# Loading the first batch's tokens and first matrix in the order TensorE uses them, by halves, with fewer warm-up products

## The chip, the cores and the metric

The kernel runs on one core of one Trainium2 chip. The metric is the device time of one execution, in microseconds (us). The core has five engines that run their own instruction streams: TensorE (PE, with its weight loads shown apart as PEld), VectorE (DVE), ScalarE (ACT), GpSimd (POOL) and SyncE (SP). Loads and stores are issued by SP, ACT and POOL and are carried by sixteen DMA engines that all three share.

## The reference

Two blocks follow each other, on 8 batches of 3008 tokens of 256 channels. The first multiplies the tokens' spectrum by a filter, the second is a feed-forward layer:

```
X = np.fft.rfft(x, axis=1)
F = (filt_r + 1j * filt_i)[None, :, :]
y = np.fft.irfft(X * F, n=x.shape[1], axis=1)     # (8, 3008, 256)

x = y.reshape(8 * 3008, 256)
h = x @ w_in                                      # (24064, 2048)
g = h - np.tanh(h)
out = g @ w_out                                   # (24064, 256)
```

## The kernel before, in words

The sequence of 3008 tokens is written as 64 times 47: token 47 q + r, with q from 0 to 63 and r from 0 to 46. The Fourier transform is done as two steps of small matrix products, one over q (for each r) and one over r. Because r and 47 - r go together, the kernel puts the 64 tokens of r on partitions 0 to 63 and the 64 tokens of 47 - r on partitions 64 to 127, for r from 0 to 23. The feed-forward layer then takes nearly all of the time: from about 80 us on, TensorE runs one product after another until the end, while the transforms of the later batches are threaded between them.

The change lies in the prologue, which handles batch 0 alone. The order of the instructions is the order of the code (the pool is opened with a manual schedule). What happens there, with the lines of the kernel before:

- Three token tiles `xs[0]`, `xs[1]`, `xs[2]` (128 partitions, 8 rows of r, 256 channels, 1 MB each) are loaded, each in four pieces: the lower 64 partitions ("low", L1181) and the upper 64 ("high", L1184), for rows 0 to 3 (k = 0) and 4 to 7 (k = 4). A low piece is 64 runs of 4 KB. A high piece goes backwards through the tokens, so it is made of runs of 1 KB. Row 0 of the upper half of `xs[0]` is set to zero instead of loaded.
- Three pieces `fh` of the first matrix `f` (128 partitions by 512 columns, 256 KB each) are loaded at L1177, one for each token tile. VectorE writes each into the tile `f0` twice, as it is (L1188) and times a column of signs (L1189).
- `warmer` (L1081) makes TensorE multiply a tile of ones with itself, 15 products, before the first real product. Each 4-byte product is two instructions in the trace.
- `first0(c)` (L1071) does the first step for token tile c: for each pair of rows four products of 128 by 128 into one bank, which ScalarE (in two places VectorE) copies out (L1074):

```
def first0(c):
    for i in range(0, 8, 2):
        r = 8 * c + i
        pf = z0("pf", [128, 2, 2, 128])
        for h in range(2):
            for k in range(2):
                nc.tensor.matmul(pf[:, h, k], xs[c][:, i + k, h * 128:h * 128 + 128],
                                 f0[:, r + k], start=True, stop=True)
        copy = V.tensor_copy if c == 2 and i % 4 else ACT.copy
        copy(turnt[:, :, :, r:r + 2], pf.rearrange("p h k n -> p h n k"))
```

- After the third `first0` come the transposes (`pq`, L1094), the second step (`pa` and `pb`, L428), the product with the filter on VectorE (L447 to L456), the way back (`pe`, L1139 and L1141), the stores of its result to DRAM (`ct`, L1145 and L483) and a load of these as `e` (L1129). The first product of the main part, `pu` (L595), needs that load.
- The filters of the first two groups are loaded by GpSimd at L1122. A one-element copy named `gate` (L1197) stands ahead of them on GpSimd and reads an element of `xs[2]`, so that they are issued only when that piece has landed. GpSimd clears three small parts of the filter tiles (L1195).
- The tiles `one` (L1191) and the first part of `mats` (L1192), needed from `pq` and `pa` on, and the first piece `raw` of the weights (L175) are loaded by SP behind its token pieces.

SP and ACT hand their loads out over eight completion semaphores in turn, in the order of the program: each load waits, on the engine that issues it, until the load eight before it on these two queues has landed. GpSimd has eight of its own.

Of the kernel before, what the change touches and what calls it, by code (L numbers as in the profile page):

```python
# [9 lines left out]
F32 = mybir.dt.float32  # L10
# [5 lines left out]
ALU = mybir.AluOpType  # L16

BATCH, SEQ, DM = 8, 3008, 256
NQ, NR = 64, 47
NA = NQ // 2  # L20
NH = (NR + 1) // 2
SG = 5
# [95 lines left out]
def kernel(  # L118
# [9 lines left out]
    nc = tc.nc  # L128
    V, G, ACT = nc.vector, nc.gpsimd, nc.scalar
    f_d, both_d, g_d, whole_d, mats_d, one_d, wide_d, pairs_d, whole_pairs_d, split_d = (  # L130
        nc.inline_tensor(v, name=n).ap()
        for v, n in zip(_consts(), ("f", "f_both", "g", "g_whole", "mats", "one", "wide",
                                    "g_pairs", "g_whole_pairs", "f_split")))
# [12 lines left out]
    def dram(t, off, dims):  # L146
        return bass.AP(tensor=t, offset=off, ap=[list(d) for d in dims])
# [478 lines left out]
    def merged(U):  # L626

        i, u = divmod(U, 4)
        b, c = groups[i]
        return u == 2 and (1 < c < NC - 1 if b == 0 else  # L630
                           c < (4 if b == BATCH - 2 else NC) and b < BATCH - 1)
# [400 lines left out]
    with tc.tile_pool(name="tr", bufs=2) as tr, tc.manual_schedule():  # L1032
# [16 lines left out]
        with tc.tile_pool(name="pro", bufs=1) as pro, \  # L1049
                tc.tile_pool(name="ps0", bufs=8, space=bass.MemoryType.PSUM) as ps0:  # L1050

            def z0(name, shape):
                return ps0.tile(shape, F32, tag="z", bufs=8, name=name)
# [3 lines left out]
            def big(shape, dtype, name):  # L1057

                return pro.tile(shape, dtype, tag="big", bufs=3, name=name)
# [4 lines left out]
# [12 lines that stand above are left out]
            def warmer(n, t=None):  # L1076

                warm = z0("warm", [128, 256])
                t = f0[:, 0:2].rearrange("p a n -> p (a n)") if t is None else t
                for _ in range(n):  # L1080
                    nc.tensor.matmul(warm, t[:, 0:128], t, start=True, stop=True)  # L1081
# [31 lines left out]
            def filters_of(g):  # L1113

                t, queue = filt[g % 3], G if g < 2 else nc.sync
                if g == last_g:
                    t = pro.tile([128, 512], I64, tag="raw", bufs=3, name="filt_end")
                    t = t.bitcast(F32).rearrange("p (v n) -> p v n", v=4)
                    ACT.mul(t[0:HB], f0.rearrange("p a n -> p (a n)")[0:HB, 0:4 * DM]
                            .rearrange("p (v n) -> p v n", v=4), 0.0)  # L1120
                for v, row, n, src in filter_rows(g):
                    queue.dma_start(t[row:row + n, v], src)  # L1122
                return t
# [38 lines left out]
            filt = [pro.tile([KM, 4, DM], F32, name=f"filt{k}") for k in range(3)]  # L1162
            f0 = pro.tile([128, NH, 128], F32, name="f0")
# [3 lines left out]
            sgn = cst.tile([128, 1], F32, name="sgn")  # L1167
            for half in range(2):
                V.memset(sgn[64 * half:64 * half + 64], 1.0 - 2 * half)
            V.memset(filt[2][:, 0], 1.0)  # L1170
            xs, began = [], []
            for c in range(3):
                lo = int(c == 0)
                xt = big([128, 8, DM], F32, "x0")
                xs.append(xt)
                fh = pro.tile([128, 8, 64], F32, tag="e1", bufs=4, name="fh")
                (ACT if c else nc.sync).dma_start(fh, f_d[:, 512 * c:512 * c + 512])  # L1177
                if lo:
                    V.memset(xt[64:128, 0], 0.0)
                for k in (0, 4):  # L1180
                    nc.sync.dma_start(xt[0:64, k:k + 4], dram(x.tensor, (8 * c + k) * DM,  # L1181
                                                              [[NR * DM, 64], [1, 4 * DM]]))
                    at = max(k, lo)
                    (ACT if c + k == 0 else G).dma_start(  # L1184
                        xt[64:128, at:k + 4], dram(x.tensor, (NR - 8 * c - at) * DM,
                                                   [[NR * DM, 64], [-DM, k + 4 - at], [1, DM]]))
                r = 8 * c
                V.tensor_copy(f0[:, r:r + 8, 0:64], fh)  # L1188
                V.tensor_scalar(out=f0[:, r:r + 8, 64:128], in0=fh,  # L1189
                                scalar1=sgn, scalar2=None, op0=ALU.mult)  # L1190
            nc.sync.dma_start(one, one_d)  # L1191
            nc.sync.dma_start(mats[:, 0:3 * KM], mats_d[:, 0:3 * KM])  # L1192
            ACT.activation(warm_b, warm_b, AF.Arctan)
            for t in filt:
                G.memset(t[0:SG, 2:4], 0.0)  # L1195
            gate = cst.tile([1, 1], F32, name="gate")
            G.tensor_copy(gate, xs[2][64:65, 0, 0:1])  # L1197
            fts = {0: filters_of(0)}

            warmer(15, filt[2][:, 0])  # L1200
            first0(0)
            first0(1)
            began.append(begun(tiles0, jobs[0], queue=nc.sync))
# [107 lines left out]
        with tc.tile_pool(name="dn", bufs=2) as dn, \  # L1311
# [73 lines left out]
            for U in range(total + 2):  # L1385
# [8 lines left out]
                if U < total:  # L1394
                    p, c = groups[i]
                    if c == 0 and u == 0 and 0 < p < BATCH - 1:
                        plan += STAGES
                    at = (2, 0) if merged(4 * i + 2) else (3, 2)
# [124 lines left out]
```

## Time and profile before

| what | value |
|---|---|
| median of three runs | 2543.22 us (2541.65 to 2544.98) |
| the profiled execution | 2542.18 us |
| its span, first to last instruction | 2540.3 us |
| PE busy in the span | 2522.6 us (99%) |
| DVE, ACT, POOL busy | 1935.6, 1694.2, 1532.0 us |
| granted TensorE clock, mean | 0.999 |

The profile is of one execution. The span is 1.9 us shorter than that execution's time; the rest lies around it. A row of the timeline gives the start, the duration, the engine, the line, the operation and how many instructions it merges; in brackets stands the idle time ahead of it and what ended it. ACTq and SPq are the instruction queues of ACT and SP, on which DMA issues stand. The rows for DMA queues name q1 for SP's loads, q10 for ACT's and q0 for GpSimd's, with the count of packets, the megabytes and the share of the sixteen engines' time.

### The profile page before, as it was taken

Reading aid. Unit: us, or ns where it says so; the run is one execution under the profiler, and the core shown is the slowest. Engines: PE = TensorE matmul, PEld = TensorE weight load, DVE = VectorE, ACT = ScalarE, POOL = GpSimd, SP = SyncE. Lnnn points to the kernel's source line nnn. Section 1 sums busy time; section 2 is a strip of 40 time slices with the busy share of each in tenths; the row PEclk is TensorE's granted clock in tenths of the full one; section 3 lists DMA queues with packets and bytes.
Section 4 is the critical chain, followed back from the end, with each engine's and each line's share of the span. In section 5 each row is a group of like instructions: output and inputs, shape, how many; then the busy total and the mean of one; then the engine's idle time right before and its main releaser. Section 6 shows DMA issues by size and latency. Waiting matters only on the chain.

```text
span 2540.3 us, 44575 instructions
## 1 busy us (share of the span) xinstructions
PE 2522.6 (99%) x17072; PEld 2173.1 (86%) x17072; DVE 1935.6 (76%) x2270; ACT 1694.2 (67%) x2551; POOL 1532.0 (60%) x1112
## 2 busy tenths in 40 slices
PE   9999999999999999999999999999999999999998
PEld 8678889888898888988888888898889888898887
DVE  6888877988678876888669886698866888555555
ACT  4666666667666766676667666666666666666665
POOL 5255665667556765676656665666655666455552
PEclk9999999999999999999999999999999999999999
DMA  9854224422343323342334322343123322110110
GB/s 245 261 150 117 65 54 100 112 65 53 86 108 91 82 69 89 80 112 59 80 87 105 87 56 72 96 111 89 36 72 84 92 66 53 26 31 19 25 22 19
DMA packets 333664, 211.37 MB, mean 83 GB/s; under 512 B 231645, under 2 KB 305531, under 8 KB 329793
## 3 DMA queue, kind: packets, MB, share of 16 engines
q1 hardware_dynamic: 319091, 184.93, 29.8%
q0 software_dynamic: 11120, 16.16, 2.3%
q10 hardware_dynamic: 3230, 7.34, 0.9%
q8 instruction: 136, 2.23, 0.4%
q14 instruction: 87, 0.71, 0.1%
HBM read 127.81 MB, written 83.39 MB: 83 GB/s over the span
## 4 chain that ended last, share of the span: by engine, by line
PE 96%; DVE 2%; DMA 1%; issue 0%; POOL 0%; ACT 0%; ACTq 0%; SPq 0%; POOLq 0%; DVEq 0%
PE o L821 44%; PE x L648 25%; PE z L648 12%; PE y L648 6%; PE pm L415 2%; PE pu L595 2%; PE pm L351 1%; PE o L883 1%; PE pf L308 1%; DMA filt<-in_filt_r_dram 1%; DMA x<-in_x_dram 0%; DMA ct<-e 0%; PE o L719 0%; PE x L719 0%; PE z L719 0%
## 5 line engine op out<-in xcount | busy, mean ns | idle before, releaser
L821 PE MATMUL o<-t,wd 128*128 128x256 f32 (+1 forms) x3008 | 762.7, 376 | 0.0
L619 POOL TENSOR_TENSOR t<-h 128x512 f32<-128x512 f32 (+1 forms) x184 | 303.6, 1650 | 707.3 <-DVE h L771 642.2
L771 DVE TENSOR_TENSOR h<-h,y 128x1024 f32<-128x1024 f32 (+1 forms) x384 | 571.0, 1487 | 156.4 <-ACT y L767 156.4
L821 PEld LDWEIGHTS o<-t,wd 128*128 128x128 f32 x3008 | 568.8, 190 | 84.5 <-POOL o L853 15.1
L648 PE MATMUL x<-tu,wu 128*128 128x256 f32 (+1 forms) x2256 | 571.4, 376 | 0.0
L821 PE MATMUL o<-h,wd 128*128 128x256 f32 (+1 forms) x2256 | 569.9, 375 | 0.2 <-DVE h L771 0.2
L648 PEld LDWEIGHTS x<-tu,wu 128*128 128x128 f32 x2256 | 427.4, 190 | 53.8 <-issue 3.9
L821 PEld LDWEIGHTS o<-h,wd 128*128 128x128 f32 x2256 | 428.3, 190 | 50.9 <-issue 0.8
L654 ACT COPY s<-x 128x512 f32<-128x512 f32 (+1 forms) x188 | 109.3, 581 | 517.4 <-PE x L648 517.3
L764 ACT ACTIVATE y<-y 128x1024 f32<-128x1024 f32 (+1 forms) x384 | 399.5, 1040 | 12.1
L767 ACT ACTIVATE y<-y 128x1024 f32<-128x1024 f32 (+1 forms) x384 | 399.8, 1041 | 4.6
L761 ACT ACTIVATE y<-h 128x1024 f32<-128x1024 f32 (+1 forms) x384 | 400.6, 1043 | 2.5 <-DVE h L697 1.7
L622 POOL TENSOR_TENSOR t<-h,t 128x512 f32<-128x512 f32 (+1 forms) x184 | 338.3, 1838 | 0.0
L620 POOL TENSOR_TENSOR t<-h,t 128x512 f32<-128x512 f32 (+1 forms) x184 | 310.5, 1688 | 14.4
L621 POOL TENSOR_TENSOR t<-h 128x512 f32<-128x512 f32 (+1 forms) x184 | 276.9, 1505 | 0.0
L654 ACT COPY u<-x 128x512 f32<-128x512 f32 (+1 forms) x376 | 214.1, 569 | 72.9 <-PE x L648 69.6
L697 DVE COPY h<-x 128x512 f32<-128x512 f32 (+1 forms) x188 | 127.6, 679 | 129.1 <-PE x L648 128.9
L689 DVE TENSOR_TENSOR h<-z,u 128x512 f32<-128x512 f32 (+1 forms) x188 | 127.2, 677 | 88.9 <-ACT u L654 88.5
L648 PE MATMUL x<-ut,wu 128*128 128x256 f32 (+1 forms) x752 | 194.0, 380 | 0.2 <-DVE h L697 0.2
L648 PE MATMUL z<-tu,wu 128*128 128x256 f32 (+1 forms) x752 | 190.2, 375 | 1.4 <-DVE h L705 1.4
L648 PE MATMUL y<-ut,wu 128*128 128x256 f32 (+1 forms) x752 | 190.1, 375 | 0.0
L648 PE MATMUL z<-ut,wu 128*128 128x256 f32 (+1 forms) x752 | 190.0, 375 | 0.0
(215 smaller groups left out, 2933.5 us busy)
## 6 DMA issues: line engine op xcount, KB each, us to landing
ft<-filt SPq DMA_DIRECT2D x28, 1024.0 KB
ct<-nn SPq DMA_DIRECT2D x56, 512.0 KB
e<-ct SPq DMA_DIRECT2D x47, 512.0 KB
a<-ct SPq DMA_DIRECT2D x112, 192.0 KB
out_dram<-ot SPq DMA_DIRECT2D x1248, 16.0 KB
x_sb<-in_x_dram SPq DMA_DIRECT2D x110, 128.0 KB
ct<-a SPq DMA_DIRECT2D x60, 128.0 KB
ct<-x_sb SPq DMA_DIRECT2D x60, 128.0 KB
```

Of the source, the lines that this page charges most:

```text
L619: by.tensor_sub(t[0], b[0][1], b[0][0])
L620: by.tensor_sub(t[1], b[1][1], t[0])
L621: by.tensor_sub(t[2], b[1][1], b[0][1])
L622: by.tensor_sub(t[3], b[1][0], t[1])
L648: nc.tensor.matmul(bank[:, k], wu[:, q - 1, (2 * u + k) * 128:(2 * u + k + 1) * 128], rhs[q - 1], start=(first and k == 0), stop=True, ski ...
L654: ACT.copy(t, X)
L697: V.tensor_copy(h[:, 2, :, 0:w], X)
L761: ACT.activation(y[k], ht[k], AF.Arctan, scale=TURN)
L764: ACT.activation(y[k], y[k], AF.Tanh, scale=BEND)
L767: ACT.activation(y[k], y[k], AF.Square, scale=SCALE, accum_out=y_sums[:, 2 * U + k // 2:2 * U + k // 2 + 1])
L771: V.tensor_mul(ht[k], ht[k], y[k])
L821: nc.tensor.matmul(product(q), wd[:, q - 1, (2 * u + k) * 128: (2 * u + k + 1) * 128], rhs[q - 1][:, k], start=(u == 0 and k == 0 and q == ...
```

## The change

The loads of the prologue are issued in another order and on other queues. The first matrix piece of tile 0 is split in two halves of four rows (128 KB each): the first is issued by SP, the second by ACT. Tile 0's second high piece moves from GpSimd to ACT, behind the second matrix half. ACT then issues the matrix pieces of tiles 1 and 2. SP issues the low pieces as before. GpSimd clears the filter tiles first, and then issues the four high pieces of tiles 1 and 2. VectorE doubles the first matrix piece in two halves. The gate reads the last token piece instead of the one before it. The warm-up is 8 products instead of 15.

```
-            for c in range(3):
-                ...
-                fh = pro.tile([128, 8, 64], F32, tag="e1", bufs=4, name="fh")
-                (ACT if c else nc.sync).dma_start(fh, f_d[:, 512 * c:512 * c + 512])
-                if lo:
-                    V.memset(xt[64:128, 0], 0.0)
-                for k in (0, 4):
-                    nc.sync.dma_start(xt[0:64, k:k + 4], dram(x.tensor, (8 * c + k) * DM,
-                                                              [[NR * DM, 64], [1, 4 * DM]]))
-                    at = max(k, lo)
-                    (ACT if c + k == 0 else G).dma_start(
-                        xt[64:128, at:k + 4], dram(x.tensor, (NR - 8 * c - at) * DM,
-                                                   [[NR * DM, 64], [-DM, k + 4 - at], [1, DM]]))
-                r = 8 * c
-                V.tensor_copy(f0[:, r:r + 8, 0:64], fh)
-                V.tensor_scalar(out=f0[:, r:r + 8, 64:128], in0=fh,
-                                scalar1=sgn, scalar2=None, op0=ALU.mult)
+            V.memset(xs[0][64:128, 0], 0.0)
+            for t in filt:
+                G.memset(t[0:SG, 2:4], 0.0)
+            def load_low(c, k, queue): ...      # the low piece, as before
+            def load_high(c, k, queue): ...     # the high piece, as before
+            def load_f(c, k, n, queue):
+                queue.dma_start(fhs[c][:, k:k + n],
+                                f_d[:, 512 * c + 64 * k:512 * c + 64 * (k + n)])
+            def doubled(c, k, n):
+                r, half = 8 * c + k, fhs[c][:, k:k + n]
+                V.tensor_copy(f0[:, r:r + n, 0:64], half)
+                V.tensor_scalar(out=f0[:, r:r + n, 64:128], in0=half,
+                                scalar1=sgn, scalar2=None, op0=ALU.mult)
+            load_f(0, 0, 4, nc.sync)
+            load_high(0, 0, ACT)
+            load_low(0, 0, nc.sync)
+            load_f(0, 4, 4, ACT)
+            load_high(0, 4, ACT)
+            load_low(0, 4, nc.sync)
+            for c in (1, 2):
+                load_f(c, 0, 8, ACT)
+            for c in (1, 2):
+                for k in (0, 4):
+                    load_low(c, k, nc.sync)
+                    load_high(c, k, G)
+            for c, k, n in ((0, 0, 4), (0, 4, 4), (1, 0, 8), (2, 0, 8)):
+                doubled(c, k, n)
...
-            for t in filt:
-                G.memset(t[0:SG, 2:4], 0.0)
-            G.tensor_copy(gate, xs[2][64:65, 0, 0:1])
+            G.tensor_copy(gate, xs[2][64:65, 4, 0:1])
-            warmer(15, filt[2][:, 0])
+            warmer(8, filt[2][:, 0])
```

How the change stands on two engines, at the start of the program. First ACT. Here `x_87` is the first token tile, `fh` a matrix piece, `warm_b` the operand of the first activation, `pf` the result of `first0`. Before:

```order
L1518 UNCONDITIONAL_BRANCH
L1184 DMA x_87<-in_x_dram 64x3x256
L1177 DMA fh<-f 128x512 x2
L1193 ACT_TABLE_LOAD
L1193 ACTIVATE warm_b<-warm_b 128x1
L1074 COPY wd<-pf 128x256x2 x8
```

and in the change:

```order
L1536 UNCONDITIONAL_BRANCH
L1183 DMA x_87<-in_x_dram 64x3x256
L1188 DMA fh<-f 128x256
L1183 DMA x_87<-in_x_dram 64x4x256
L1188 DMA fh<-f 128x512 x2
L1213 ACT_TABLE_LOAD
L1213 ACTIVATE warm_b<-warm_b 128x1
L1074 COPY wd<-pf 128x256x2 x8
```

Two loads now stand between ACT's first load and the matrix pieces of tiles 1 and 2: half a matrix piece and the second high piece of tile 0.

Then GpSimd, whose rows at this place were (`x_87`, `x_97` and `x_106` are the three token tiles, `filt_77` to `filt_79` the filter tiles):

```order
L1184 DMA x_87<-in_x_dram 64x4x256
L1184 DMA x_97<-in_x_dram 64x4x256 x2
L1184 DMA x_106<-in_x_dram 64x4x256 x2
L1195 MEMSET filt_77 5x512
L1195 MEMSET filt_78 5x512
L1195 MEMSET filt_79 5x512
L1197 COPY gate<-x_106 1x1
```

and are in the change (the token tiles are now `x_87`, `x_88` and `x_89`):

```order
L1175 MEMSET filt_77 5x512
L1175 MEMSET filt_78 5x512
L1175 MEMSET filt_79 5x512
L1183 DMA x_88<-in_x_dram 64x4x256 x2
L1183 DMA x_89<-in_x_dram 64x4x256 x2
L1215 COPY gate<-x_89 1x1
```

GpSimd's five loads became four, behind the three clears, and none of them is for the first token tile any more.

More of the change, by code (lines that the diff above doesn't have):

```diff
@@ L1170 @@
             V.memset(filt[2][:, 0], 1.0)
-            xs, began = [], []
-            for c in range(3):
-                lo = int(c == 0)
-                xt = big([128, 8, DM], F32, "x0")
-                xs.append(xt)
-                fh = pro.tile([128, 8, 64], F32, tag="e1", bufs=4, name="fh")
-                (ACT if c else nc.sync).dma_start(fh, f_d[:, 512 * c:512 * c + 512])
-                if lo:
-                    V.memset(xt[64:128, 0], 0.0)
-                for k in (0, 4):
-                    nc.sync.dma_start(xt[0:64, k:k + 4], dram(x.tensor, (8 * c + k) * DM,
-                                                              [[NR * DM, 64], [1, 4 * DM]]))
-                    at = max(k, lo)
-                    (ACT if c + k == 0 else G).dma_start(
-                        xt[64:128, at:k + 4], dram(x.tensor, (NR - 8 * c - at) * DM,
-                                                   [[NR * DM, 64], [-DM, k + 4 - at], [1, DM]]))
-                r = 8 * c
-                V.tensor_copy(f0[:, r:r + 8, 0:64], fh)
-                V.tensor_scalar(out=f0[:, r:r + 8, 64:128], in0=fh,
-                                scalar1=sgn, scalar2=None, op0=ALU.mult)
+            xs, began = [big([128, 8, DM], F32, "x0") for _ in range(3)], []
@@ new lines, with load_low, load_high @@
+            fhs = [pro.tile([128, 8, 64], F32, tag="e1", bufs=4, name="fh") for _ in range(3)]
+            V.memset(xs[0][64:128, 0], 0.0)
+            for t in filt:
+                G.memset(t[0:SG, 2:4], 0.0)
+            def load_low(c, k, queue):
+                queue.dma_start(xs[c][0:64, k:k + 4], dram(x.tensor, (8 * c + k) * DM,
+                                                           [[NR * DM, 64], [1, 4 * DM]]))
+            def load_high(c, k, queue):
+                at = max(k, int(c == 0))
+                queue.dma_start(xs[c][64:128, at:k + 4],
+                                dram(x.tensor, (NR - 8 * c - at) * DM,
+                                     [[NR * DM, 64], [-DM, k + 4 - at], [1, DM]]))
```

## The prediction

> **What bounds the kernel now.** I read the page first, then the busy time by stretches, then the start of the program engine by engine.
>
> ```profile
> span 2540.3 us, 44575 instructions
> ...
> 25.00:30.00 5.00, 5.00 (x33) 4.36 (x32) 4.84 (x8) 3.23 (x6) 2.63 (x5) 1.00 0.88 231
> ...
> 45.00:50.00 5.00, 4.97 (x24) 3.90 (x23) 4.86 (x7) 2.29 (x5) 3.38 (x4) 1.00 1.07 304
> ...
> 80.00:90.00 10.00, 10.00 (x31) 5.71 (x31) 8.98 (x18) 5.46 (x11) 1.45 (x2) 1.00 0.94 311
> ...
> 300.00:2500.00 2200.00, 2200.00 (x15196) 1916.36 (x15195) 1669.48 (x1881) 1492.88 (x2242) 1371.45 (x957) 1.00 0.29 71
> ```
>
> The columns after the length are PE, PEld, DVE, ACT and POOL, then clock, DMA share and GB/s. From 80 us on PE is busy the whole of these stretches, so the rest of the program can only be moved as a whole, by the moment at which its first product `pu` starts. The prologue ahead of it is a chain without slack: DVE is busy 4.84 of 5 us at 25 and 4.86 at 45.
>
> ```profile
> 1.45 9.44 PE L1081 MATMUL warm<-filt 120*128 120x256 f32 x30 [1.45 <-DVE filt L1170]
> ...
> 10.72 10.88 PE L1071 MATMUL pf<-f,x 128*128 128x128 f32 x96
> ...
> 22.54 1.06 PE L1094 MATMUL pq<-one_sb,wd 128*120 128x128 f32 x8 [0.94 <-ACT wd L1074]
> ...
> 23.64 0.69 DVE L1099 COPY a<-pq 120x512 f32<-120x512 f32 x1 [1.20 <-PE pq L1094]
> ...
> 73.68 2.23 DMA e<-ct
> 75.91 0.14 issue
> 76.05 0.33 PE pu L595 x4
> ```
>
> PE runs the warm-up and the first step back to back to 21.60 (10.72 + 10.88). What follows hangs on that: the transposes, DVE's copy at 23.64, DVE's busy stretch, the round trip through DRAM, `pu` at 76.05. So I take a shift of 21.60 to reach the end one for one.
>
> Was PE waiting for data when it began at 10.72, or only for its own warm-up?
>
> ```profile
> 4.20 0.62 DVE L1188 COPY f<-fh 128x512 f32<-128x512 f32 x1 [2.42 <-DMA fh<-f]
> ...
> 11.10 0.43 DVE L1188 COPY f<-fh 128x512 f32<-128x512 f32 x1 [5.54 <-DMA fh<-f]
> 11.44 0.48 DVE L1189 TENSOR_SCALAR f<-fh,sgn 128x512 f32<-128x512 f32 x1
> ...
> 15.12 0.43 DVE L1188 COPY f<-fh 128x512 f32<-128x512 f32 x1 [3.20 <-DMA fh<-f]
> ...
> 6.82 0.33 SPq L1191 DMA_DIRECT2D one_sb<-one  x1
> ...
> SPq L1191 <- DMA x<-in_x_dram: 0.6, 1, 0.6
> ...
> 15.40 0.19 POOL L1197 COPY gate<-x 1x1 f32<-1x1 f32 x1 [8.91 <-DMA x<-in_x_dram]
> ...
> L1184 POOL DMA_DIRECT2D x<-in_x_dram x5: 618/631/815, 1.3 to 3.9; - x5
> ...
> DMA to landing us min/median/max: 7.5/10.6/14.0
> ```
>
> The three matrix pieces landed at about 4.2, 11.1 and 15.1. SP's load of `one` waits for tile 0's first low piece, eight loads before it, so that piece landed at 6.8. GpSimd's first piece (tile 0, k = 4) landed at 1.3 + 7.5 = 8.8, its fourth at 15.4 (the gate), its last at 3.9 + 14.0 = 17.9. PE uses each sixth of the first step for 10.88 / 6 = 1.81 us, the last from 19.8. So PE started about 4 us after the first half's data, and the last data came 1.9 us ahead of use.
>
> **The change part by part.** *Warm-up.* 14 of 30 instructions go.
>
> ```profile
> 70.00 3.62 PE L1081 MATMUL warm<-f 128*128 128x256 f32 x16
> ...
> 76.05 0.33 PE L595 MATMUL pu<-gt,e 64*64 64x64 f32 x4 [2.42 <-DMA e<-ct]
> ...
> 77.79 1.56 PE L1374 MATMUL pt<-mats_sb 120*120 120x256 f32 x6
> ```
>
> At full rate 16 of these take 3.62 us, 0.226 each, so 30 would take 6.8; the first warm-up took 9.44, thus 2.65 us of it were lost to a slow start, though the clock column says 1.00 there. The instructions that go are the last and fast ones: 14 x 0.226 = 3.2 us. PE is free for tile 0 at 10.72 - 3.2 = 7.5, after its data (6.8), and its first half is done at 9.3.
>
> *The second high piece of tile 0.* This is where I expect the change to turn. It moves from the head of GpSimd's queue, where it landed at 8.8, to third place in ACT's. How fast does ACT's queue move beside two others?
>
> ```profile
> q0 software_dynamic: 214, 0.70, 41.2%
> q1 hardware_dynamic: 214, 0.70, 39.9%
> q10 hardware_dynamic: 193, 0.36, 22.3%
> ...
> q10 hardware_dynamic: 166, 0.16, 34.8%
> ...
> q1 hardware_dynamic: 134, 0.26, 32.3%
> ...
> q10 hardware_dynamic: 210, 0.20, 16.7%
> ```
>
> The first three rows are of 7 to 13 us, when all three queues were full: nearly the same count of packets, but half the bytes on q10, whose matrix pieces go in 2 KB and the others' tokens in 4 KB. Each queue gets its turn by packets: 193 in 6 us are 32 per us. In the change ACT's queue holds 1 KB runs: 128 for the matrix half and 64 x 4 = 256 for the high piece. The last row (0 to 5 us) says that the 192 of its first load are through by 5. Then 384 packets at 32 per us last until 17.0 if both rivals stay full. They don't quite: SP and GpSimd move 0.70 MB in 6 us each, a 256 KB piece in 2.2 us. GpSimd's four pieces start about 1.5 us later than its five did, behind the clears:
>
> ```profile
> 4.55 1.93 POOL L1195 MEMSET filt<- 5x512 f32 x3
> ```
>
> so at about 5.3, and take 4 x 2.2 = 8.8 us, a tenth less with ACT's shorter packets (9 KB for a round instead of 10): until 13.2. By then ACT, at 32 x 10 / 9 = 35 per us, has passed 35 x 8.2 = 287, and the last 97 go within half a microsecond. Allowing a slower first microsecond beside SP, I put the last packet at 14.4. Landing comes later: matrix piece 0 had its packets through by 3.0 (134 in the row of 0 to 3 us) and DVE saw it at 4.2, so 1.2 us. The high piece lands at 15.6. Bounds: 5 + 384 / 83 + 1.2 = 10.8, at the rate that ACT had from 3 to 5 us beside SP alone (the row with 166 in 2 us), and 18.2 at 32 per us throughout. I take 15.6 because the 7 to 13 row is of the same three full queues.
>
> The Trainium skill, page "DMA: Bandwidth & Descriptors", section "Queues, rings and completion order", says that an engine takes turns between queues by packets and typically drains 9 to 17 descriptors as one packet. Read so, several 1 KB runs would go in one turn and the high piece would be near the early bound. Here the 2 KB and 4 KB packets took turns one for one, which speaks for single runs.
>
> *Matrix pieces 1 and 2* stand behind it: 0.52 MB at the 0.29 MB per us that the three queues move together (1.76 MB in 6 us), so 0.9 us each: landing at 16.5 and 17.4 instead of 11.1 and 15.1. Doubling takes 0.9 us (the rows at 11.10 and 11.44), so tile 1 may start at 17.4, tile 2 at 18.3.
>
> *PE then.* Idle from 9.3 to 15.6. Five sixths of the first step remain, 9.05 us: 15.6 + 9.05 = 24.7 at full speed (second half of tile 0 to 17.4, tile 1 just ready). Against 21.60 that is 3.1 us later.
>
> *The rate after the gap.* PE started slow at the program's begin; after 2.42 us of idleness at 73.6 it was fast (`pt`: 6 in 1.56 us, 0.26 at most). A gap of 6.3 us lies between. The slow start took twice the lost 2.65 us, so about 5.3 us of work, to end; a gap longer than that I take to be long enough to undo it. The price is then again 2.65 us, with 0 as the other bound: end of the first step 27.4, 5.8 us late.
>
> The Trainium skill, page "TensorE: Matmul & The Clock Gate", Part 1, states that an idle window of about 3.4 us throttles TensorE and that about 3.4 us of work releases it. By that figure the gap throttles too but costs half of 3.4, 1.7 us, and the sum would be 26.4, 4.8 us late (an estimate from that page).
>
> *Covered edits.* The two added DVE halves cost some 0.3 us, in DVE's waits (2.42 and 5.54 us). ACT's second big matrix load now waits for ACT's first load, and holds back the activation table and first copy behind it:
>
> ```profile
> 2.63 1.28 ACT L1193 ACT_TABLE_LOAD   x1 [2.63 <-issue]
> ...
> 11.81 7.05 ACT L1074 COPY wd<-pf 128x512 f32<-128x512 f32 x8 [7.68 <-PE pf L1071]
> ...
> 23.68 0.66 ACT L181 ACTIVATE top<-raw 128x512 f32<-128x512 f32 x1
> ...
> 11.09 0.41 SPq L1192 DMA_DIRECT2D mats_sb<-mats  x1
> ...
> 15.12 0.61 SPq L175 DMA_DIRECT2D raw<-in_moe_w_in_dram  x1
> ...
> 15.54 7.44 DMA filt<-in_filt_r_dram
> ...
> 29.15 1.22 DVE nn L447
> ```
>
> the load lands at about 5, the table is in by 7, the first copy is due at 8.5. Without that cover it would cost up to 1 us. SP's `mats` moves from 11.1 to the high piece's landing (15.6) and `raw` behind it from 15.1 to matrix piece 1's (16.5); `raw` is used at 23.68 and later, `mats` after `pq`, and both uses shift with PE. The gate now waits for GpSimd's last piece, which I put at 15.0 (13.2 plus 1.8), as late as today's gate; the filters need 7.4 us and are used at 29.15. All nothing. Later loads wait for the same loads as before, eight back.
>
> **Sum.** Against the profiled execution, 2542.18 + 5.8 = 2548.0. That execution was 1.0 below the median of the three, 2543.22, against which the result is read: 2549.0. I predict 2549.
>
> **The rivals.** *TensorE doesn't throttle in the gap*: 2543.2 + 3.1 = 2546.3. For it, the fast products after 2.42 us of idleness; against it, the gap is 2.6 times as long.
>
> *ACT's queue drains several runs a turn*: the high piece lands at 10.8, tile 0 ends at 12.6, matrix piece 1 follows (128 packets at 32 per us from 9.6, so 13.6 plus 1.2 plus 0.9 of doubling) at 15.7, tile 1 ends at 19.3 with matrix piece 2 (17.4 + 0.9) in time, and the step at 22.9: 1.3 late, 2544.5. Both gaps are then about 3 us or less. This is what the section on queues of the Trainium skill's page "DMA: Bandwidth & Descriptors" would make of it.
>
> *The forecast's opposite: only the warm-up held PE.* If the high piece lands by 12.5, and the doubled matrix pieces 1 and 2 are there by 14.3 and 18.0, PE is bound by the last token piece alone, at 17.9 as now: 17.9 + 1.81 = 19.7, 1.9 us earlier, 2541.3. For it, PE did start 4 us after its data; against it, ACT's queue carries 832 packets instead of 448 and the equal turns above. The deciding point is 12.5 for the high piece.
>
> **How the numbers follow.** About 0.2%, 5.1 us, is what a measurement of this kernel can tell from no change. Forecast 0.62, no throttling 0.14, several runs a turn 0.16, earlier 0.08. The forecast's own case spreads over 4.5 us (landing at 18.2 at the latest: 18.2 + 9.05 + 2.65 = 29.9, 8.3 late, 2551.5; with the smaller price of a short slow stretch near 2547), and about three quarters of it lie over 2548.3. So slower by over 0.2% gets 0.49, with a little from the no-throttling case's late landings 0.50, faster by as much 0.02 (even the earlier case gives 1.9), the rest 0.48. The range runs from 2543.5, which takes in the several-runs case, to 2552, and leaves out the earlier case and the tails.
>
> **What would show it.** In the profile of the changed kernel: warm-up 16 instructions, ended by 8; 16 products of the first step, then PE idle until 15 or 16 with DMA of `x` named; VectorE's doubling of piece 1 near 16.5 instead of 11.1; q10 with the same packet count as q1 but a quarter of the bytes from 7 to 13 us; the products after the gap at 0.2 us apart and then at 0.11; `pu` near 82 instead of 76.05, and from there the same gaps. Wrong would be: a gap under 3.5 us, matrix piece 1 before 14, or a shift of the first step's end that `pu` doesn't repeat.

## The result, and the profile after

| | before | after |
|---|---|---|
| median | 2542.26 us (2540.58 to 2544.99, 12 runs) | 2548.15 us (2545.42 to 2550.37, 12 runs) |
| the profiled execution, its span | 2542.18, 2540.3 us | 2547.76, 2545.9 us |

The medians differ by 5.9 us; the ratio is 1.0021, with a 95% interval of 1.0013 to 1.003. So the change makes the kernel slower. The forecast was 2549.0. The time is right, but the trace reaches it by another sum than mine.

TensorE's timeline of the changed kernel (start, duration, line, operation, count; in brackets the idle time ahead and what ended it), from the start and then from the end of the prologue:

```profile
1.45 6.74 PE L1081 MATMUL warm<-filt 120*128 120x256 f32 x16 [1.45 <-DVE filt L1170]
8.02 1.95 PE L1071 MATMUL pf<-f,x 128*128 128x128 f32 x16
14.27 10.88 PE L1071 MATMUL pf<-f,x 128*128 128x128 f32 x80 [4.29 <-issue]
...
27.92 1.96 PE L428 MATMUL pa<-a,mats_sb 120*120 120x256 f32 x4 [0.78 <-DVE a L1099]
29.68 1.91 PE L428 MATMUL pb<-a,mats_sb 120*120 120x256 f32 x4
...
80.91 0.33 PE L595 MATMUL pu<-gt,e 64*64 64x64 f32 x4 [2.05 <-DMA e<-ct]
81.51 1.15 PE L595 MATMUL pu<-gt,e 64*64 64x64 f32 x60 [0.27 <-DMA e<-ct]
82.59 3.67 PE L1392 MATMUL pt<-mats_sb 120*120 120x256 f32 x8
86.09 1.68 PE L719 MATMUL x<-ut,wu 128*128 128x448 f32 x4
```

Four of these rows in the kernel before:

```profile
24.39 1.12 PE L428 MATMUL pa<-a,mats_sb 120*120 120x256 f32 x4 [0.78 <-DVE a L1099]
25.34 1.03 PE L428 MATMUL pb<-a,mats_sb 120*120 120x256 f32 x4
...
77.79 1.99 PE L1374 MATMUL pt<-mats_sb 120*120 120x256 f32 x8
79.77 1.77 PE L719 MATMUL x<-ut,wu 128*128 128x448 f32 x4
```

The first step ends at 14.27 + 10.88 = 25.15 instead of 21.60, 3.5 us late. `pu` starts at 80.91 instead of 76.05, 4.9 late. The products `x` behind `pt` start 6.3 late. The spans differ by 5.6: from `x` to the end the changed kernel took 2459.8 us and the one before 2460.5. This last part takes 2459.1 to 2460.7 us in eleven of the twelve profiles of this document, so the 0.7 lies within its spread. So some two fifths of the loss come after the first step. The rows `pa`, `pb` and `pt` show where: eight `pt` products took 3.67 us, and 1.99 us before. The changed kernel by stretches of 3.41 us (the first figure after the length is PE's busy time; the column before the DMA share is the granted clock):

```profile
11.00:14.41 3.41, 0.14 (x1) 0.17 (x2) 0.00 (x0) 0.00 (x0) 0.00 (x0) 1.00 1.04 287
14.41:17.83 3.42, 3.42 (x17) 3.35 (x17) 0.82 (x2) 0.80 (x1) 0.00 (x0) 0.50 1.03 243
17.83:21.24 3.41, 3.41 (x32) 3.41 (x32) 0.82 (x2) 2.91 (x4) 3.41 (x7) 1.00 0.82 245
24.65:28.07 3.42, 1.70 (x14) 1.30 (x13) 1.64 (x3) 1.58 (x3) 1.75 (x4) 1.00 1.05 326
28.07:31.48 3.41, 3.41 (x9) 2.46 (x10) 1.99 (x4) 0.59 (x1) 2.31 (x4) 0.50 0.78 159
...
79.27:82.68 3.41, 1.50 (x65) 1.36 (x65) 0.44 (x1) 0.00 (x0) 0.00 (x0) 1.00 0.59 185
82.68:86.09 3.41, 3.41 (x8) 2.60 (x9) 2.63 (x6) 1.15 (x2) 0.00 (x0) 0.50 1.01 241
```

The clock drops to half for whole stretches of 3.41 us, and all of them start on one grid (from 14.41 to 28.07 it is four stretches, from there to 82.68 sixteen). Each follows a stretch in which PE was half idle or more. At full work such a stretch costs half its length, 1.7 us. The Trainium skill, page "TensorE: Matmul & The Clock Gate", Part 1, speaks of a free-running window of about 3.4 us, after which TensorE drops to half or returns; this trace agrees.

When did the data come? VectorE's copies of matrix pieces 0b (the second half), 1 and 2, then what SyncE's queue waited for (total, times, longest) and when its loads went out. The load of `one` stands eight loads behind tile 0's second high piece:

```profile
6.91 0.29 DVE L1193 COPY f<-fh 128x256 f32<-128x256 f32 x1 [3.21 <-DMA fh<-f]
...
16.79 0.43 DVE L1193 COPY f<-fh 128x512 f32<-128x512 f32 x1 [9.32 <-DMA fh<-f]
...
18.66 0.43 DVE L1193 COPY f<-fh 128x512 f32<-128x512 f32 x1 [1.05 <-DMA fh<-f]
```

```profile
SPq L1211 <- DMA x<-in_x_dram: 6.4, 1, 6.4
```

```profile
14.19 0.33 SPq L1211 DMA_DIRECT2D one_sb<-one  x1
```

The high piece landed at 14.2, and TensorE took up tile 0's second half at 14.27. Piece 1 arrived at 16.8 instead of 11.1. Its doubling ended at 17.6, and tile 1's first product started at 17.68. From there the last two thirds of the step took 25.15 - 17.68 = 7.5 us, 0.2 more than before.

Two causes meet at 17.6, and this trace alone can't part them. The 16 product instructions of tile 0's second half ran from 14.27 to 17.68 without a gap, 0.21 us apart instead of 0.11. So the high piece's landing together with the half clock held tile 1 back as long as piece 1 did, and either of the two without the other would have ended the step within 0.2 us of where it ended. The experiments take them apart.

### The profile page after: what moved, and what is told of

It reads as the page before. It is cut to its first block, busy times and chain, and to the rows that moved or that the text cites. A ratio compares the mean times of both kernels' runs of the same rounds, so it can differ in the third digit from the quotient of the medians.

```text
span 2545.9 us, 44551 instructions
## 1 busy us (share of the span) xinstructions
PE 2524.7 (99%) x17058; PEld 2174.8 (85%) x17058; DVE 1935.6 (76%) x2272; ACT 1694.3 (67%) x2551; POOL 1531.3 (60%) x1111
## 3 DMA queue, kind: packets, MB, share of 16 engines
q8 instruction: 136, 2.23, 0.4%
## 4 chain that ended last, share of the span: by engine, by line
PE 97%; DVE 1%; issue 1%; DMA 0%; POOL 0%; ACT 0%; ACTq 0%; SPq 0%; POOLq 0%; DVEq 0%
PE o L821 44%; PE x L648 25%; PE z L648 12%; PE y L648 6%; PE pm L415 2%; PE pu L595 2%; PE o L883 1%; PE pm L351 1%; PE pf L308 1%; PE pf L1071 0%; PE o L719 0%; PE pe L1141 0%; PE warm L1081 0%; PE pe L1139 0%; PE x L719 0%
## 5 line engine op out<-in xcount | busy, mean ns | idle before, releaser
L620 POOL TENSOR_TENSOR t<-h,t 128x512 f32<-128x512 f32 (+1 forms) x184 | 310.5, 1688 | 14.4
```

The costliest lines, as they stand in the source:

```text
L620: by.tensor_sub(t[1], b[1][1], t[0])
```

## The experiments

Each time is compared with runs of the kernel before, made beside it on the same chip; their medians were 2542.5 to 2542.9.

**Fifteen warm-up products again** (the rest of the change stays):

```
-            warmer(8, filt[2][:, 0])
+            warmer(15, filt[2][:, 0])
```

> The change with 15 warm-up products again; loads as in the change. Theory (the late first-matrix piece of tile 1, which waits in ACT's queue behind tile 0's second high piece, sets the first step's end; the number of warm-ups doesn't): tile 1's piece is doubled near 17.6 us as in the change, so the first step ends at 24.9 instead of 25.14, and the time is about 2545.6, 3.4 over the kernel before, plus 0 to 3.4 for slow-clock stretches of 1.7 each. PE's gap shrinks to about 1.7 us, so no slow stretch at 14 to 18. Rival (the loss comes from the warm-up being cut, through the gap and the slow clock): the time is back within 1 us of the kernel before, 2542 to 2543.

Measured: 2547.61 us (2545.22 to 2548.57), ratio 1.0017 [1.0008, 1.0026]. TensorE's timeline:

```profile
1.45 9.37 PE L1081 MATMUL warm<-filt 120*128 120x256 f32 x30 [1.45 <-DVE filt L1170]
...
13.52 2.02 PE L1071 MATMUL pf<-f,x 128*128 128x128 f32 x16 [0.91 <-issue]
17.88 7.41 PE L1071 MATMUL pf<-f,x 128*128 128x128 f32 x64 [2.34 <-DVE f L1194]
```

No stretch of the prologue is slow here, and yet the first step ends at 25.29, as late as in the change: 17.88 is piece 1 once more, this time without the clock. This profiled run took 2545.22 us, 3.0 more than the profile of before. So the late data alone are worth some 3 us, and the shorter warm-up is not their cause.

**Eight warm-up products in the kernel before** (the same edit the other way round):

> The kernel before with 8 warm-up products; loads as before. Theory: the first half of tile 0 starts at 8.0 instead of 10.7, and then PE follows the data of the kernel before (second half of tile 0 at 9.8, tile 1 at 12.0 and 14.0, tile 2 at 16.05 and 18.3), so the first step ends near 20.15, 1.45 earlier, all gaps under half a microsecond, no slow stretch from them: 2540.8. Rival (fewer warm-ups cost the clock): a slow stretch in the first step, its end at 21.6 or later, 2542.5 to 2545.

Measured: 2543.48 us (2541.62 to 2545.25), ratio 1.0 [0.9991, 1.0009]. The first step ends at 20.84, 0.8 earlier, but `pu` starts at 76.30, not earlier. TensorE's timeline and the waits between 54 and 84 us:

```profile
13.05 7.79 PE L1071 MATMUL pf<-f,x 128*128 128x128 f32 x64 [0.31 <-DMA x<-in_x_dram]
...
76.30 0.33 PE L595 MATMUL pu<-gt,e 64*64 64x64 f32 x4 [2.35 <-DMA e<-ct]
```

```profile
DVE xy L452 <- DMA filt<-in_filt_i_dram: 2.9, 1, 2.9
```

This row is not among the waits of before. VectorE now comes to a filter group before its loads have landed. That this wait is what takes the 0.8 us fits the rows, but was not shown by itself. The half clock comes at `pu` and `pt` as well (77.05 to 80.46 us: eight `pt` in 2.87 us). An earlier first step brings nothing here; the expectation missed both.

**Tile 0's second high piece back on GpSimd, at the head of its queue**, with the clears behind that one load and ahead of the other four:

```
-            for t in filt:
-                G.memset(t[0:SG, 2:4], 0.0)
...
-            load_high(0, 4, ACT)
+            load_high(0, 4, G)
+            for t in filt:
+                G.memset(t[0:SG, 2:4], 0.0)
```

> The change with one load moved back: tile 0's second high piece is issued by GpSimd, first, ahead of the clears; all else as in the change. Theory: ACT's queue loses 256 packets of 1 KB, the piece lands near 9, the first-matrix pieces of tiles 1 and 2 near 12 and 15.5, the first step ends near 20.2, bound by the last token pieces: 2540.8, 1.5 under the kernel before. Rival (the pieces of the first matrix are late because all the queues together are full, whoever carries the piece): first-matrix piece 1 lands after 15, the step ends after 23.5, 2544.5 or more.

Measured: 2544.85 us (2541.4 to 2546.16), ratio 1.0006 [0.9997, 1.0015]. Piece 1 is seen at 11.17 again, and the first step ends at 21.40:

```profile
9.18 2.02 PE L1071 MATMUL pf<-f,x 128*128 128x128 f32 x16 [0.25 <-DMA x<-in_x_dram]
13.61 7.79 PE L1071 MATMUL pf<-f,x 128*128 128x128 f32 x64 [2.40 <-DMA x<-in_x_dram]
```

The wait of 2.40 us is now for tile 1's high piece, behind the clears. So the place of this one load decides the end of the first step. The time did not come down to the expected one. In this profile `pu` starts at 79.51, late, behind two longer waits (between 54 and 84 us) and a slow stretch from 70.33 to 73.75:

```profile
DVE xy L452 <- DMA filt<-in_filt_i_dram: 5.8, 2, 4.6
ACT e L1144 <- DMA ct<-e: 5.1, 2, 4.3
```

**All of GpSimd's side as before**: the high piece at its head and all five loads ahead of the clears. Of the change remain the halves of piece 0 and the 8 warm-up products.

> The change with GpSimd's side undone: tile 0's second high piece back at the head of GpSimd's queue, all five pieces ahead of the clears, as before. The halves of matrix piece 0 and the 8 warm-up products stay. Theory (the first step was late because matrix piece 1 stood behind 384 short packets in ACT's queue): piece 1 is there by 11.5, the first step ends at 20 to 21, earlier than 21.6, the whole loss of the change is gone. But the prologue's middle (filters by 62 us, the round trip through DRAM) does not move with it, so pu starts at 76.0 to 76.6 and the time is 2542 to 2543.5. Rival 1 (a shift of the first step's end passes one for one to pu): pu at 74.5 to 75.0, 2541. Rival 2 (the loss lies in the halves or the warm-up count): step end at 23 or later, 2545 or more.

Measured: 2544.2 us (2542.74 to 2545.16), ratio 1.0005 [0.9996, 1.0014]. TensorE's timeline:

```profile
9.67 2.02 PE L1071 MATMUL pf<-f,x 128*128 128x128 f32 x16 [1.07 <-DMA x<-in_x_dram]
12.98 7.77 PE L1071 MATMUL pf<-f,x 128*128 128x128 f32 x64 [1.29 <-DVE f L1192]
...
75.51 0.33 PE L595 MATMUL pu<-gt,e 64*64 64x64 f32 x4 [2.48 <-DMA e<-ct]
76.28 1.83 PE L595 MATMUL pu<-gt,e 64*64 64x64 f32 x60 [0.44 <-DMA e<-ct]
78.04 2.90 PE L1392 MATMUL pt<-mats_sb 120*120 120x256 f32 x8
```

The first step ends at 20.75 (expected 20 to 21), and the loss is gone within what the measurement can tell. Of the 0.86 us that the step gained, `pu` keeps 0.54, which lies between the theory and rival 1. The stretch from 76.5 to 79.91 has the half clock (60 `pu` in 1.83 us instead of 1.15, `pt` 2.90 instead of 1.99) and takes 1.6 us. The time came out 0.7 above the expected range. The halves and the warm-up count do not make the loss, but bring nothing either.

**Only the clears moved back** behind GpSimd's loads; the high piece stays third on ACT.

> The change with only GpSimd's three clears moved back behind its loads; tile 0's second high piece stays third on ACT. GpSimd's pieces start 1.4 us sooner. Theory (ACT's queue is too long in front of matrix piece 1, whoever else loads): piece 1 is still seen by VectorE at 16.5 to 18, the first step ends at 25 to 26.5, the time is 2547 to 2549. Rival (the order of the clears made the loss, because GpSimd's pieces now run against ACT's): piece 1 by 14.5, step end by 23.5, 2545 or less.

Measured: 2548.86 us (2546.73 to 2551.61), ratio 1.0026 [1.0015, 1.0036]. TensorE, VectorE, and two stretches:

```profile
7.41 1.95 PE L1071 MATMUL pf<-f,x 128*128 128x128 f32 x16
15.86 11.14 PE L1071 MATMUL pf<-f,x 128*128 128x128 f32 x80 [6.50 <-DMA x<-in_x_dram]
...
17.14 0.43 DVE L1191 COPY f<-fh 128x512 f32<-128x512 f32 x1 [9.25 <-DMA fh<-f]
```

```profile
13.16:16.58 3.42, 0.72 (x3) 0.75 (x4) 0.00 (x0) 0.00 (x0) 1.79 (x4) 0.50 1.03 252
16.58:19.99 3.41, 3.41 (x18) 3.41 (x17) 1.72 (x4) 1.14 (x2) 3.41 (x7) 0.50 0.94 217
```

The order of the clears is not the cause. Here the prediction's picture of the first step comes out as it stands: a gap of 6.5 us until the high piece lands at 15.9, then a slow clock. 15.86 + 9.05 would be 24.9; the step ends at 27.00, half a microsecond past the expected range, so the slow clock costs 2.1 us where it isn't hidden: two stretches in a row were slow, and PE worked in the last 4.1 us of them.

**Piece 1 issued by SyncE**, behind tile 0's low pieces (one run):

```
-            for c in (1, 2):
-                load_f(c, 0, 8, ACT)
+            load_f(1, 0, 8, nc.sync)
+            load_f(2, 0, 8, ACT)
```

> The change with one load moved: first-matrix piece 1 is issued by SP behind tile 0's low pieces instead of by ACT behind tile 0's second high piece, which stays on ACT. Theory (two things hold the first step: that high piece, landed at 14.2, and the matrix piece behind it, doubled at 17.6): piece 1 lands near 10, only the high piece is left, and the step ends near 14.2 + 9.1 = 23.3 with a fast clock, or 25.0 with a slow stretch behind the gap. Rival (piece 1 is late because everything is): landing after 15 and the step's end at 25.

Measured: 2547.94 us in one run, span 2546.1.

```profile
14.42 11.43 PE L1071 MATMUL pf<-f,x 128*128 128x128 f32 x80 [5.47 <-issue]
...
11.45 0.43 DVE L1193 COPY f<-fh 128x512 f32<-128x512 f32 x1 [4.36 <-DMA fh<-f]
```

Piece 1 is early again (11.45), and the step still ends at 25.85: now the high piece holds it, which landed at 14.4 (14.2 in the change), and the clock is half from 12.33 to 19.16:

```profile
12.33:15.75 3.42, 1.33 (x6) 1.36 (x7) 0.00 (x0) 0.00 (x0) 0.00 (x0) 0.50 1.04 288
15.75:19.16 3.41, 3.41 (x18) 3.41 (x17) 0.84 (x2) 1.60 (x2) 1.67 (x4) 0.50 1.06 209
```

Without that it would end at 14.42 + 9.05 = 23.5. So two loads behind each other were late, and taking away the later one uncovers the other and the clock.

**The high piece in runs of 4 KB** (64 of them, taken forward through the tokens, so other tokens than the step needs; one run):

```
-            load_high(0, 4, ACT)
+            ACT.dma_start(xs[0][64:128, 4:8], dram(x.tensor, (NR - 7) * DM, [[NR * DM, 64], [1, 4 * DM]]))
```

> The change with tile 0's second high piece still third in ACT's queue, but read in 64 runs of 4 KB (forward, so other tokens) instead of 256 of 1 KB. If queues take turns by packets, one for one: 64 packets at 30 per us, the piece is through 2.1 us after its start at 6, lands by 10, first-matrix piece 1 lands near 13.5 and piece 2 near 17.3, the first step ends near 22. If queues share by bytes or time, whatever the packets: landing at 14 and 16.8 as in the change and the step's end at 25.

Measured: 2545.01 us in one run.

```profile
9.69 2.02 PE L1071 MATMUL pf<-f,x 128*128 128x128 f32 x16 [1.10 <-DMA x<-in_x_dram]
15.22 8.94 PE L1071 MATMUL pf<-f,x 128*128 128x128 f32 x64 [3.51 <-DVE f L1194]
...
14.34 0.43 DVE L1193 COPY f<-fh 128x512 f32<-128x512 f32 x1 [7.49 <-DMA fh<-f]
```

The same bytes in a quarter of the packets: the second half of tile 0 starts at 9.69 instead of 14.27, and piece 1 is there at 14.34 instead of 16.79. So the short runs make most of the high piece's lateness and 2.4 of piece 1's 5.7 us. The rest of piece 1's I put down to the bytes of the two loads ahead of it; that was not tried by itself. The step ends at 24.16, some 1.6 us of it by a slow stretch from 15.03 to 18.44. This lies between the two expectations.

**Filler products in the change's gaps** (9 products in the first step's gap, 3 around `pq`, 4 more ahead of `pu`), to keep the clock up:

```
+                    if c == 0 and i == 4:
+                        warmer(9)
...
+            warmer(2)
...
+            warmer(1)
...
-            warmer(8)
+            warmer(12)
```

> The change with TensorE kept busy in its waits by products whose result nobody reads: 9 between the two halves of tile 0, 2 ahead of the transposes, 1 ahead of the second step, and 12 instead of 8 ahead of the main part. Theory (the change costs about 3 us by late data, and the rest of its 5.6 by slow-clock stretches of 3.4 us, each losing up to 1.7, which an idle TensorE brings on): no slow stretch at 14 to 18, 28 to 31 or 82 to 86 us; the first step still ends near 25.0, because first-matrix piece 1 is late; median near 2545.5, runs within about 2.5 us of each other. Rival (the slow stretches are not what costs the rest, or idleness is not what brings them): 2548 as the change, with the same spread of 5 us.

Measured: 2546.89 us (2545.51 to 2550.48), ratio 1.0017 [1.0008, 1.0026]. The mean clock of its runs rose to 0.9987 from the change's 0.9969, yet the time cannot be told from the change's. Its profile shows why at the first step:

```profile
14.24 2.02 PE L1073 MATMUL pf<-f,x 128*128 128x128 f32 x16 [1.68 <-issue]
18.13 9.04 PE L1073 MATMUL pf<-f,x 128*128 128x128 f32 x64 [1.86 <-DVE f L1196]
```

The waits for the high piece and for piece 1 still leave PE only 1.56 us of work between 15.21 and 18.63. So the slow stretch was not avoided but came one stretch later, from 18.63 on, where no wait covers it, and the step ends at 27.17 instead of 25.15. The later slow stretches are gone (`pt` takes 1.99 us), and `x` starts at 85.36, 0.7 earlier than in the change. This run was nevertheless one of the longest, 2550.32 us: its part from `x` to the end took 2463.1 us, at the full clock, and what made it longer is not known.

**The small fillers in the kernel before** (without the 9):

> The kernel before with the same fillers except the first (2 ahead of the transposes, 1 ahead of the second step, 12 instead of 8 ahead of the main part). Theory (the spread of the kernel before, 2540 to 2546, is also slow-clock stretches that come or don't with the phase of the clock's windows): median 2541.5, spread under 3 us. Rival (the spread is something else, such as DMA): median 2542.5 to 2543 and the same spread of 6 us.

Measured: 2544.19 us (2541.66 to 2545.74), ratio 1.0005 [0.9996, 1.0014]. No gain; the spread did not become narrower. In its profile the clock stays up and `pu` starts at 76.40, 0.35 late, behind the longer warm-up ahead of it.

**Eight warm-up products in the kernel before, and the load `x1`** (the next batch's first tile) **moved behind the filter loads**, so that the filters come first:

```
-                if g == 2:
-                    x1 = load_x(big([128, 8, DM], F32, "x1"), 1, 0, 8)
...
                         turned_in(fts[last_g])
+                        x1 = load_x(big([128, 8, DM], F32, "x1"), 1, 0, 8)
```

> The kernel before with 8 warm-up products and with the load of batch 1's tokens x1 (1 MB, SP) moved behind the filter loads of groups 4 to 6. Theory (8 warm-ups end the first step 0.76 us earlier, but DVE then waits 2.9 us for a filter of group 4 that SP issues behind x1, and the gain is lost): the wait for that filter goes, pu starts near 75.3 instead of 76.3, median about 2542.0 and 1.5 under that of 8 warm-ups alone. Rival (the filter is late because all DMA queues are full, not because of x1 ahead of it): the wait stays, 2543.5 as with 8 warm-ups alone.

Measured: 2549.14 us (2548.43 to 2551.41), ratio 1.0025 [1.0014, 1.0035], a clear miss. The first step ends at 20.18, the best of all, and then, by the waits between 40 and 84 us and TensorE's timeline:

```profile
ACT e L1144 <- DMA ct<-e: 9.5, 2, 8.8
```

```profile
69.67 4.97 PE L1227 MATMUL pf<-x,f 128*128 128x256 f32 x14 [3.67 <-DMA x<-in_x_dram]
...
82.11 2.19 PE L595 MATMUL pu<-gt,e 64*64 64x64 f32 x61 [4.00 <-DMA e<-ct]
```

The filter wait is gone, but 1 MB of tokens now travels with the stores of `e`, and the half clock comes twice (69.91 to 73.32 and 80.15 to 86.97). ScalarE waits 8.8 us for a store to free its buffer, TensorE 3.7 us for `x1`, and `pu` starts 6 us late. A load moved out of one wait made two others.

## Why the prediction was right

- **PE free at 7.5, first half done at 9.3**: 8.0 and 10.0. The slow start took longer in this run (16 product instructions in 6.74 us); in the other kernels with 8 warm-up products the first half began at 6.63 to 7.41. What sets this moment stands below, under the slow clock.
- **The high piece at 15.6** (10.8 to 18.2): 14.2. Right in place and size, and the cause that I gave, equal turns by packets, failed for runs of 1 KB. The queues of the changed kernel from 7 to 9 us, while the high piece was under way (packets, megabytes, share):

```profile
q10 hardware_dynamic: 189, 0.19, 46.2%
q1 hardware_dynamic: 49, 0.17, 36.0%
q0 software_dynamic: 42, 0.11, 23.1%
```

  ACT's queue got about four packets of 1 KB for one of the others' 4 KB. The rival with several runs a turn was right on that, and wrong on the landing that I drew from it (10.8). The Trainium skill, page "DMA: Bandwidth & Descriptors", section "Queues, rings and completion order", gives 9 to 17 descriptors a turn as typical; four of 1 KB is what these rows show, so the direction agrees and the size does not. Nor is four fixed: from 3 to 5 us, with SP's queue alone beside it, ACT's got 187 packets while SP's got 96. The trace's packet records show how 14.2 came about. By their count, the 320 packets ahead of the high piece had started by 6.1, not by 9.0 as at my 32 per us, and 236 of its own 256 by 10.2; the last 20 started between 10.3 and 12.9, among those of piece 1. The sixteen engines reported the load done between 9.2 and 14.2. A load is there when its slowest engine is done, and I had no term for that. An early start, a fast drain and a long tail happened to give nearly my time, so its nearness is luck. (That the last 97 packets would go within half a microsecond followed from no row either; at the 83 per us of my early bound they take 1.2.)
- **Pieces 1 and 2 at 16.5 and 17.4**: 16.8 and 18.7. The run with 15 warm-up products shows that piece 1 alone is enough to hold the step, the run with piece 1 on SyncE that the high piece and the half clock together are too. Piece 2's lateness cost nothing: its first use came at 21.4.
- **The gap from 9.3 to 15.6**: 4.3 us long instead of 6.3, and PE then worked at half rate until piece 1 was ready.
- **The slow clock, 2.65 us**: that a slow clock follows the gap held; its size and its place in the sum did not. The size was read from the program's start, which is another case. There the warm-up instructions are 0.43 us apart and then 0.22, and in all twelve traces the change of pace falls on the trace's first record of a granted clock, at 4.8 to 7.6 us (6.9 before, 7.6 in the change). Ahead of it the clock column's 1.00 stands for no record. So the start runs at half rate up to that moment and loses half of the time since 1.45 us, while a gap later on brings a stretch of 3.41 us, 1.7 us at full work, the lower price that I had only beside the sum. In the first step of the change the slow clock added 0.2 us instead of 2.65, since the wait for piece 1 ran through the same time; where nothing covered it (the clears moved back) it cost 2.1. It then came twice more, at `pa`/`pb` and at `pt`, and I had priced neither. The step ended at 25.15 instead of 27.4, 3.5 late instead of 5.8; the two later stretches made up the difference. So the number came out because two errors met: one term hidden, two left out. That the time is right is luck in this respect.
- **No throttling, 2546.3**: its 3.1 us is the size of the data's part, as the run with 15 warm-up products showed (3.0). It left out the clock, so its time did not come.
- **The shift passes to `pu` and the end**: 3.5 at the step's end, 4.9 at `pu`, 5.6 in the span. A loss passes on to `pu` nearly one for one, slow stretches apart: in the run with 15 warm-up products, where none is slow, 3.7 at the step's end are 3.3 at `pu`. For a gain it fails: 0.8 us of an earlier step became nothing in one kernel, 0.86 became 0.54 in another.
- **The covered edits** were covered: with only the halves, the warm-up count and the later gate left, nothing was lost that could be measured. In the change GpSimd's last piece landed at 17.8 instead of the 15.0 that I had put, so the gate opened 2.4 us later than before; no wait of VectorE for a filter shows in that trace.

How much is the clock's in the medians? Over the 69 runs of before that were made beside the experiments the mean clock is 0.9986, and the mean time rises from 2542.2 (clock 0.999) to 2543.6 (0.998), 1.4 us for a thousandth. The change's 12 runs have 0.9969. The difference, 1.7 thousandths, is worth about 2.4 us by that slope. That leaves 3.5 for the late data. This is an estimate from a correlation, but it meets the 3.0 of the profile without slow stretches.

**Which idle places bring the half clock?** The twelve traces answer this nearly. Cut the first 90 us of each into stretches of 3.41 us on the grid that its clock records give. Of 280 stretches at full clock, 13 had PE busy for 1.50 us or less, and the half clock followed every one; 263 had it busy for 1.73 us or more, and it followed none. Of the four between, it followed three (1.56, 1.69, 1.70 us) and not the fourth (1.57). So it is not the length of a gap that counts but whether about half of one stretch is idle. The wait ahead of `pu` shows it: 2.42 us of idleness in the kernel before lie across a grid line (PE busy 1.83 and 2.23 us in the two stretches), and `pt` is fast; 2.48 us with GpSimd's side as before fall into one stretch (0.55 us busy), and `pt` is slow. That is why the fast products behind 2.42 us of idleness said less against a slow clock than the prediction took from them.

**What stays open.** The grid's phase differs from run to run; no run here set it. No version that was run beats the kernel before.

## What to carry to other kernels

Ordering loads by first use is not enough: count what stands ahead of each load in its own queue, in bytes and in packets, and ask which second load is late behind the first. An earlier first step was worth half a microsecond at best here, since later waits for loads took the rest; moving one of those loads cost more than it gave. Where two terms of a sum run through the same time, add only what sticks out, and look for the same mechanism at every later idle place.

## What the runs showed of the hardware

- The half clock came in whole stretches of 3.41 us on a fixed grid, after stretches in which PE had been busy for 1.70 us or less (16 cases in the first 90 us of twelve traces), and never after one at the full clock with 1.73 us or more (263 cases). In the change the two later ones cost 1.6 us at `pa`/`pb` and 1.5 at `pt` where they stood.
- At the program's start product instructions ran at half pace, 0.43 us apart instead of 0.22, until the first clock record, 4.8 to 7.6 us into the span.
- From 7 to 9 us, with three queues full, runs of 1 KB got about four turns for one of 4 KB (189 packets against 49 and 42; 0.19, 0.17 and 0.11 MB); with two queues, from 3 to 5 us, about two for one (187 against 96). In the kernel before 2 KB and 4 KB took turns one for one (193 packets against 214 and 214 in 6 us).
- The sixteen engines of one load of 256 packets reported it done between 9.2 and 14.2 us.
